# A fused retention and GELU kernel: the written-out order of its 1459 steps is exchanged for another

## Chip, cores and metric

The kernel runs on one core of a Trainium2 chip. The metric is the time of one execution on the device in microseconds (us). Three runs of the kernel before took 286.53, 286.94 and 287.16 us; their median is 286.94. A further execution was profiled.

The core has a matrix engine (PE, with its weight loads shown as PEld), a vector engine (DVE), a scalar engine (ACT), GpSimd (POOL) and a sync engine (SP). Each works through its own list of instructions in order, and semaphores tie the lists together. SP does no arithmetic here: it issues DMAs.

## What is computed

Retention (attention with a causal decay in place of a softmax) over 8 batches, 8 heads, 576 positions and head size 64, then a two-layer network with the tanh form of GELU over the 4608 tokens:

```python
scores = q @ k.transpose(0, 1, 3, 2) / sqrt(64)
rel = pos[:, None] - pos[None, :]
ret = scores * where(rel >= 0, gamma ** rel, 0)   # gamma = 1 - 2 ** (-5 - head)
x = (ret @ v).transpose(0, 2, 1, 3).reshape(4608, 512)
out = gelu_tanh(x @ w_in) @ w_out                 # w_in 512 x 2048, w_out 2048 x 512
```

Inputs and output are float32; the matrix work is done in float16 with sums in float32.

## The kernel before, in words

**Units.** The sequence of a batch is cut into four chunks of 128 positions and a tail of 64, so there are 40 units, u = 5 * batch + chunk. Step `L,u,n` loads q (n = 0), k (1) or v (2) of a unit into a page of SBUF (L227; the tails by two small DMAs, L233; the first two chunks of batches 0 and 1 are loaded as one wide pair, L210 and L215). All pages are loaded by SP. There are 7 sets of pages for units up to 15 and 3 from then on.

Steps `q`, `k`, `v` cast a page to float16, q and v with a factor of decay (L436, wide pairs L451, k by L281 or L279). The last letter names the engine: `v` DVE, `a` ACT, `g` POOL; with no letter q goes to DVE and v to POOL. `D,u` transposes q and k of a unit by one DMA that SP issues (L495). The wide pairs are transposed on PE instead (`t`, L505) and copied out by `y`.

`B,u,w` is the attention's matrix work (lines 541 to 586): it finishes unit w (the earlier state times q at L541, the masked scores times v at L586), and starts unit u (key times value at L565, the scores from the transposed q and k at L575). `m` masks the scores (L703), `a` adds to the running state in float32 (L725, L723), `o` decays it (L733), `z` casts it to float16 in two halves (L281, L279, L743), `Z` zeroes those buffers (L402). `x` moves a finished unit into `xT` (L598 on ACT, L596 on DVE). For wide pairs `X`, `Y`, `R` take the place of `B`.

**The network.** Tokens are taken in 9 blocks t of 512. For blocks 0 to 2 the first layer is `N,t,fc,part` (8 matmuls, L769), followed by `F` (GELU on ACT, L777). For blocks 3 to 8 it is done with 7 instead of 8 products of half-size blocks: `A,t,g,i` (4 matmuls each, L968) for four groups g, with sums of blocks of `xT` (`s`, DVE) and of w_in (`U`, DVE). The products gather in two PSUM banks; `l` copies or adds an intermediate stage out of the bank before the next product adds on top (L279 on ACT, L281 and L829 on DVE), and `f` applies GELU (L986). The second layer of block 0 and of the last 256 tokens is plain (`O`, L795; `P`, L998). All other pairs of 256 tokens use 7 products `W,t,pair,i` (8 matmuls each, L871), with sums of GELU blocks (`H`, DVE) and of w_out (`T`, DVE) and with `V` to carry the results out of PSUM (L829, L279). `e` and `E` copy a plain result, `S` and `Q` store (L787, SP).

The weights are loaded by POOL (`I` for the 8 pieces of w_in, `J` for those of w_out, L250). `K,n` are n filler matmuls (L1014) that write nothing that is read. `g`, `c`, `w` make tables.

**What sets the order.** The steps stand as words in one string, `ORDER`, written out by hand or by a search, and nothing reorders them. A loop at the end of the kernel calls one function per word, and each puts its instructions at the end of the list of its engine:

```python
for step_ in ORDER.split():
    name, *args = step_.split(",")
    do[name](*[int(a) if a.lstrip("-").isdigit() else a for a in args])
```

So the string gives the order on each engine by itself. How two engines run against each other follows at run time from the semaphores, which the framework derives from the tiles that are written and read. Buffers are rings: four for the cast q and k, four for v, four for the transposed pairs, two PSUM banks for the first layer and two for the second.

Of the kernel before, what the change touches and what calls it, by code (L numbers as in the profile page):

```python
# [28 lines left out]
F,1,0,0 N,1,2,0 F,1,2,0 O,0,5 Y,7,0 L,9,1 v,7,v X,7 J,5,g J,4,g Z,0,g O,0,6 J,6,g O,0,7 q,9,g
e,0,1,a F,1,4,0 m,7,0 o,6,1 z,6,1,v O,0,10 O,0,11 e,0,2,a k,9,g a,7,1 z,7,1,g a,8,1 N,1,14,0 D,9 R,7  # L30
B,9,-1 O,0,0 O,0,1 O,0,2 N,1,10,0 O,0,3 O,0,12 O,0,13 T,1,1,v T,2,1,v O,0,14 T,4,1,v F,1,10,0
z,8,1,g F,1,14,0 H,1,0,3,v K,0 x,8 K,0 K,0 T,1,0,v L,10,1 L,10,2 K,0 v,10,v L,11,2 e,0,0,a L,13,1
T,3,0,v x,7 K,0 N,1,2,1 F,1,2,1 k,10,g K,0 L,10,0 q,10,g W,1,0,1 V,1,0,0,a L,11,0 q,11 i,4,v O,0,15
# [1053 lines left out]
```

## Time and profile before

| | before |
|---|---|
| median of 3 runs | 286.94 us (286.53 to 287.16) |
| the profiled execution | 287.18 us |
| its span, first to last instruction | 285.5 us |
| DVE, ACT, POOL busy | 79%, 62%, 41% of the span |
| instructions in the profile | 9676 |
| DMA | 49.77 MB, of which 44.97 MB on SP's queue |

The page says for each engine how long it was busy; the slices cut the span into 40 equal parts, each digit being tenths. "Idle before, releaser" in a row is the time in which the engine waited just before the instruction, and what ended that. A row of the timeline gives start, duration, engine, line, operation, output and inputs, their shape, and a count. A PE row's duration contains the pipeline's drain: starts of successive matmuls, not durations, give PE's pace. For a DMA the row of its issue gives the time that SP took for issuing, and "to landing" the time from the start of the issue until the data is there.

### The profile page before, as it was taken

The page shows a single profiled execution, that of the slowest core. Times are in us where ns is not written, and L with a number is a line of the kernel's source. Part 1 is how long each engine was busy: PE and PEld are TensorE (multiplying, and loading weights), DVE is VectorE, ACT ScalarE, POOL GpSimd, SP SyncE. Part 2 cuts the span into 40 slices and gives each one's busy share as a digit, 9 for nine tenths or more (in the row PEclk, how much of TensorE's full clock was granted, in tenths as well). Part 3 has the DMA queues.
Part 4 walks back from the last instruction along what each step waited for, and adds up shares of the span by engine and source line. Part 5 has one row for each costly group of instructions (what it writes and reads, how often), then busy time and mean ns, then how long its engine had stood idle before and what let it go on. Part 6 is the DMA issues. An engine that isn't in the chain of part 4 may idle for free. (4 is left out here: it accounts for less than half of the span.)

```text
span 285.5 us, 9676 instructions
## 1 busy us (share of the span) xinstructions
PE 275.1 (96%) x4016; PEld 230.7 (81%) x4016; DVE 224.4 (79%) x463; ACT 177.2 (62%) x341; POOL 117.1 (41%) x184
## 2 busy tenths in 40 slices
PE   3999999999999999899999999999999999999995
PEld 1567877568888888888888888888888888888874
DVE  7796273998987789678979998998989986976730
ACT  4265654245576776657777678867777576755611
POOL 5749580525424535392585393707251224000000
DMA  7999999979999999989999989999963521202112
GB/s 223 284 236 257 253 221 182 208 174 190 219 205 199 232 206 163 250 177 202 197 205 248 199 199 172 161 216 210 194 179 76 129 79 54 76 0 77 73 76 73
DMA packets 136427, 49.77 MB, mean 174 GB/s; under 512 B 118208, under 2 KB 130880, under 8 KB 136384
## 3 DMA queue, kind: packets, MB, share of 16 engines
q1 hardware_dynamic: 132032, 44.97, 73.9%
q0 software_dynamic: 4352, 4.20, 9.0%
q8 instruction: 31, 0.51, 0.8%
q14 instruction: 12, 0.10, 0.1%
HBM read 36.70 MB, written 9.44 MB: 162 GB/s over the span
## 5 line engine op out<-in xcount | busy, mean ns | idle before, releaser
L871 PEld LDWEIGHTS <-ssum 128*128 128x128 f16 x480 | 46.8, 98 | 5.5
L769 PE MATMUL bank<-xT,w_in_sb 128*128 128x256 f16 x384 | 47.0, 273 | 0.6 <-DMA w_in_sb<-in_moe_w_in_dram 0.6
L777 ACT ACTIVATE gT<-bank 128x512 f16<-128x512 f32 x48 | 28.3, 597 | 28.5 <-PE bank L769 28.3
L871 PE MATMUL bank<-tsum,ssum 128*128 128x256 f16 x360 | 45.7, 273 | 0.0
L968 PE MATMUL bank<-pages 128*128 128x256 f16 x288 | 42.1, 273 | 0.3 <-ACT pages L279 0.3
L769 PEld LDWEIGHTS <-w_in_sb 128*128 128x128 f16 x384 | 36.3, 98 | 7.2 <-DMA w_in_sb<-in_moe_w_in_dram 1.2
L968 PEld LDWEIGHTS <-pages 128*128 128x128 f16 x384 | 36.6, 98 | 5.4 <-issue 0.7
L871 PEld LDWEIGHTS <-gT 128*128 128x128 f16 x360 | 35.1, 98 | 4.3 <-issue 0.2
L279 ACT COPY hc<-bank 128x512 f32<-128x512 f32 x39 | 22.8, 585 | 23.4 <-PE bank L968 21.4
L436 POOL TENSOR_TENSOR qk<-pages,dec 128x512 f16<-128x512 f32 (+1 forms) x26 | 26.8, 1034 | 21.4 <-PE x L541 7.9
L829 DVE TENSOR_TENSOR hc<-hc,bank 128x512 f32<-128x512 f32 x43 | 29.5, 685 | 6.6 <-PE bank L968 4.3
L281 POOL CAST sz<-s 64x256 f16<-64x256 f32 x42 | 19.1, 454 | 33.5 <-DVE s L725 24.4
L871 PE MATMUL bank<-w_out_sb,gT 128*128 128x256 f16 x240 | 31.1, 273 | 0.0
L968 PEld LDWEIGHTS <-w_in_sb 128*128 128x128 f16 x288 | 27.2, 98 | 3.9 <-issue 0.2
L968 PE MATMUL bank<-xT,w_in_sb 128*128 128x256 f16 x192 | 28.8, 273 | 0.0
L436 POOL TENSOR_TENSOR v<-pages,dec 128x512 f16<-128x512 f32 (+1 forms) x23 | 22.9, 1003 | 12.2 <-PE bank L968 6.1
L986 ACT ACTIVATE gT<-hc 128x512 f16<-128x512 f32 x43 | 26.8, 629 | 1.2 <-DVE hc L829 1.1
L281 POOL CAST qk<-pages 128x512 f16<-128x512 f32 (+1 forms) x22 | 13.7, 631 | 32.1 <-DMA pages<-in_k_dram 19.6
L829 DVE TENSOR_TENSOR ssum<-gT 128x1024 f16<-128x1024 f16 x30 | 23.0, 772 | 1.2 <-ACT gT L777 0.8
L598 ACT ACTIVATE xT<-x 128x512 f16<-128x512 f32 (+1 forms) x38 | 20.5, 546 | 4.9 <-PE x L586 3.8
L829 DVE TENSOR_TENSOR ost<-u,bank 128x256 f32<-128x256 f32 x45 | 18.5, 416 | 6.1 <-PE bank L871 5.8
L279 ACT COPY pages<-bank 128x512 f32<-128x512 f32 x29 | 16.9, 582 | 9.9 <-PE bank L968 9.6
(113 smaller groups left out, 485.9 us busy)
## 6 DMA issues: line engine op xcount, KB each, us to landing
out_dram<-ost SPq DMA_DIRECT2D x35, 256.0 KB, 2.9
pages<-in_q_dram SPq DMA_DIRECT2D x32, 256.0 KB, 4.6
pages<-in_k_dram SPq DMA_DIRECT2D x24, 256.0 KB, 4.4
pages<-in_v_dram SPq DMA_DIRECT2D x24, 256.0 KB, 4.6
pages<-in_k_dram SPq DMA_DIRECT2D x4, 512.0 KB, 9.6
pages<-in_v_dram SPq DMA_DIRECT2D x4, 512.0 KB, 10.0
w_in_sb<-in_moe_w_in_dram POOLq DMA_DIRECT2D x8, 256.0 KB, 8.1
w_out_sb<-in_moe_w_out_dram POOLq DMA_DIRECT2D x8, 256.0 KB, 7.1
```

What stands on the lines that cost most here:

```text
L279: nc.scalar.copy(out=o, in_=i)
L281: (nc.vector if eng == "v" else nc.gpsimd).tensor_copy(out=o, in_=i)
L436: eng.tensor_tensor(out=out, in0=s["raw"][:, i, 0:n], in1=dec[:, i // 2, s["j"], 0:n].unsqueeze(2).to_broadcast([128, n, D]), op=ALU.mult,)
L598: nc.scalar.activation(out=o, in_=i, func=AF.Copy, bias=0.0, scale=1.0)
L769: nc.tensor.matmul(hps[:, i, :], w_in_sb[:, ct, 128 * (fc + i) : 128 * (fc + i) + 128], xT[:, ct, TB * t % XR + lo : TB * t % XR + hi], st ...
L777: nc.scalar.activation(out=gTs[t][:, fc : fc + TB // (hi - lo), lo:hi], in_=h.pop((t, fc, lo)), func=AF.Gelu_apprx_tanh, bias=0.0, scale=1.0,)
L829: (nc.vector if eng == "v" else nc.gpsimd).tensor_tensor(out=out, in0=a, in1=b, op=op)
L871: nc.tensor.matmul(p["ps", bank][:, HN * col : HN * col + HN], a[:, k], b[:, k], start=(k == 0 and i in (1, 6)), stop=(k == HK - 1), skip_ ...
L968: nc.tensor.matmul(p["ps", bank][:, n], w[:, c, 128 * n : 128 * n + 128], x[:, c], start=(n == 0 and c == 0 and i in (1, 2, 5)), stop=(c = ...
L986: nc.scalar.activation(out=gTs[t][:, f : f + 2, o : o + 256], in_=p["ps", 0] if i == 0 else p["c", i], func=AF.Gelu_apprx_tanh, bias=0.0, ...
```

## The change

Only the string differs (it is a line shorter, so that the lines of the changed kernel's code are lower by 1). Both hold 1459 words. Apart from the fillers the words are the same but for the letter of the engine: 104 words have another engine, and nearly all have another place. The fillers go from 36 matmuls to 32, and before the first matrix step of the attention from 17 to 9. In the summary below, counts of words by engine:

| steps | DVE | ACT | POOL |
|---|---|---|---|
| V, results out of PSUM | 83 to 87 | 22 to 18 | |
| z, casts of the state | 4 to 8 | 21 to 19 | 31 to 29 |
| Z, zeroing | 1 to 5 | | 5 to 1 |
| k, cast of k | 6 to 5 | 8 to 13 | 22 to 18 |
| q, cast of q | 10 to 13 | | 26 to 23 |
| v, cast of v | 11 to 12 | | 25 to 24 |
| l, stages out of PSUM | 76 to 77 | 68 to 67 | |
| x, units into xT | 3 to 4 | 37 to 36 | |
| y, copies of transposes | 4 to 5 | 6 to 5 | |
| e, plain results | 0 to 2 | 5 to 3 | |

The diff, cut to the beginning, the places of the transposes of units 12, 14, 18, 20, 21, 22 and 24, the start of block 5, and the end:

```diff
-K,5 L,0,1 L,0,0 q,0 K,3 Z,5,g K,5 K,4 I,1,g k,0,a t,0,k,h t,0,q,h L,2,0 q,2 y,0,k,v Z,3,g L,0,2
-v,0,g g K,4 y,0,q,a Y,0,1 I,0,g L,4,0 q,4 t,2,q,h y,2,q,a m,0,1 I,3,g I,2,g X,0 a,0,1 Z,1,g K,6
...
-W,1,0,7 m,10 B,11,10 x,10 F,1,0,1 D,12 L,18,0 U,2,0 N,1,6,1 v,13,v V,1,0,1,v U,4,1 a,11,0 z,10,1,g
...
-H,1,1,3,v L,16,0 N,2,4,0 D,14 W,1,0,3 F,2,12,0 V,1,0,6,v z,12,1,a L,18,2 N,2,8,0 V,1,1,0,a W,1,1,2
...
-N,2,14,1 D,18 m,16 S,1,0 v,17,g F,2,14,1 W,2,0,1 z,15,1,g B,17,16 V,2,0,0,a V,1,1,4,v o,16,1 a,17,0
...
-v,19,g V,2,0,4,v W,2,1,1 l,3,1,3,v f,3,0,3 A,3,1,7 A,3,1,5 D,20 v,20,g B,20,19 a,20,0 l,3,1,2,a
...
-D,21 H,3,0,3,v W,2,1,2 l,3,2,0,a A,3,2,6 S,1,2 j,4,a l,3,1,5,v f,3,1,2 L,23,1 a,20,1 v,21,g z,20,1,g
...
-D,22 f,3,2,1 v,24,g W,2,1,4 x,20 W,2,1,5 A,3,3,6 l,3,3,1,a A,3,3,2 S,2,0 m,21 B,22,21 L,25,0
...
-f,4,1,0 D,24 A,4,1,5 l,4,1,4,v W,3,0,3 A,4,2,1 l,4,2,0,v W,3,1,2 q,27,g A,4,1,3 l,4,1,5,v D,25
...
-A,4,3,3 z,27,0,g s,5,1 s,5,2 W,4,0,1 A,5,0,6 s,5,3 l,4,3,5,v s,5,4 l,5,0,1,a V,3,1,6,v m,27 v,28,g
-A,5,0,2 L,31,2 V,4,0,0,a L,33,1 A,5,0,7 l,5,0,3,v A,5,0,5 l,5,0,2,a A,5,0,4 f,5,0,0 S,3,2 q,30,g
...
-S,8,0 f,8,2,3 l,8,3,5,v O,8,10 f,8,3,3 P,2 O,8,11 e,8,2,a E,2,v Q,2 P,1 E,1,a P,0 Q,1 E,0,a S,8,2
-Q,0
+L,0,0 Z,2,v K,1 K,1 K,0 K,6 Z,4,v I,0,g Z,5,v I,1,g g K,1 L,0,1 k,0,a K,0 L,2,1 t,0,k,h y,0,k,v K,5
+q,0,g t,0,q,h L,0,2 v,0,g Z,1,v Z,0,v K,3 k,2,v y,0,q,a Y,0,1 X,0 m,0,1 a,0,1 K,7 Y,0,0 Z,3,g I,2,g
+t,2,k,o I,3,g K,1 z,0,1,a w L,2,0 q,2 I,4,g I,5,g I,6,g c t,2,q,h K,3 L,4,0 a,1,1 o,1,1 y,2,q,a
+L,2,2 m,0,0 R,0 y,2,k,v Y,2,0 m,2,0 x,1 x,0 K,4 q,4,g L,5,0 t,4,q,o z,1,1,a L,4,1 L,4,2 N,0,2,0
...
+x,10 L,13,1 V,1,0,1,v k,13,a T,4,1,v k,12,g D,12 z,11,0,a L,13,2 L,15,0 H,1,1,1,v H,1,1,2,v
...
+q,16,g a,13,1 D,14 F,2,12,0 m,13 B,14,13 U,4,1 m,14 L,17,0 q,17 U,3,0 k,16,a L,16,2 v,16,v x,13
...
+D,18 m,16 N,2,8,1 z,16,0,a F,2,10,1 x,15 B,17,16 F,2,8,1 S,1,0 q,19 V,2,0,0,a N,2,2,1 a,17,0 a,17,1
...
+S,1,3 z,17,0,a B,18,17 L,20,2 x,17 H,2,0,4,v W,1,1,3 W,2,0,2 L,22,0 k,20,g F,2,2,1 D,20 L,21,2
+A,3,0,2 v,19,v s,3,1 l,3,0,0,a s,3,2 A,3,0,6 V,1,1,6,v S,1,2 W,2,0,6 v,20,g V,2,0,2,v s,3,3 a,18,0
...
+l,3,2,4,v a,20,1 f,3,2,1 A,3,2,4 f,3,2,0 D,21 V,2,1,1,v k,23,v A,3,2,3 q,23,g V,2,1,3,v v,21,g
...
+D,22 z,20,1,g B,22,21 x,21 A,3,3,7 l,3,3,2,a A,3,3,5 W,2,1,3 f,3,3,1 L,24,2 v,24,g S,2,1 a,22,0
...
+A,4,1,3 z,23,1,g A,4,2,1 W,3,1,2 v,25,g D,24 V,3,0,6,v L,26,1 l,4,1,5,v D,27 A,4,2,2 m,23 l,4,2,0,a
...
+l,5,0,0,a V,3,1,6,v W,4,0,1 f,4,2,2 A,5,0,6 A,5,0,2 l,5,0,1,a l,5,0,3,v f,4,3,3 A,5,0,7 A,5,0,5
+s,5,4 S,3,3 l,5,0,2,a L,32,1 A,5,0,4 L,29,2 V,4,0,0,a H,4,0,2,v f,5,0,0 W,4,0,2 l,5,0,4,v A,5,0,3
...
+V,8,0,4,v i,0,a V,8,0,5,v S,8,1 W,8,0,3 V,8,0,6,v S,8,0 O,8,8 O,8,9 f,8,3,2 f,8,2,2 P,1 E,1,v S,7,3
+O,8,10 O,8,11 e,8,2,v S,8,2 P,0 E,0,a Q,1 P,2 E,2,a Q,0 Q,2
```

More of the change, by code (lines that the diff above doesn't have):

```diff
@@ L29 @@
[L29 to L33, printed above, removed]
-e,0,3,a L,12,2 T,2,0,v L,14,1 L,9,2 K,0 K,0 U,1,1 U,2,1 v,11,v L,11,1 k,11,v N,1,4,1 T,3,1,v D,10
```

198 lines of the change are left out of this document (100 added, 98 removed).

## Prediction

> **What bounds the kernel now.** I read the page's busy times and slices, the waits of the matrix engine, and then the issues on SP's queue.
>
> ```profile
> PE 275.1 (96%) x4016; PEld 230.7 (81%) x4016; DVE 224.4 (79%) x463; ACT 177.2 (62%) x341; POOL 117.1 (41%) x184
> PE   3999999999999999899999999999999999999995
> POOL 5749580525424535392585393707251224000000
> DMA  7999999979999999989999989999963521202112
> ...
> PE sk L565 <- POOL v L436: 0.7, 1, 0.7
> PE sk L575 <- DMA qkT<-qk: 0.3, 1, 0.3
> PE bank L968 <- ACT pages L279: 0.3, 1, 0.3
> ```
>
> The first four lines are the page, the last three all waits of PE from 30 us to the end. PE is busy 96% of the span and after 30 us it stands still for 1.3 us by name. The matrix work is the same multiset of steps after the change, so the time moves only by PE's start-up, by waits like these three, and by the tail. The DMA line says what comes second: 9 in nearly every slice up to two thirds of the span. POOL has room; its slack costs nothing.
>
> SP alone issues the page loads (L227, L233), the transposes of q and k (L495) and the stores (L787), one after the other. The issues of the stretch 60 to 160 us:
>
> ```profile
> pages<-in_q_dram SPq DMA_DIRECT2D x16, 256.0 KB, 4.6
> out_dram<-ost SPq DMA_DIRECT2D x14, 256.0 KB, 2.9
> pages<-in_k_dram SPq DMA_DIRECT2D x14, 256.0 KB, 4.4
> pages<-in_v_dram SPq DMA_DIRECT2D x14, 256.0 KB, 4.7
> pages<-in_q_dram SPq DMA_DIRECT2D x8, 64.0 KB, 4.5
> pages<-in_v_dram SPq DMA_DIRECT2D x6, 64.0 KB, 4.3
> pages<-in_k_dram SPq DMA_DIRECT2D x6, 64.0 KB, 3.3
> qkT<-qk SPq DMA_TRANSPOSE x18, 4.3
> ...
> 100.00:120.00 20.00, 18.92 (x334) 16.87 (x332) 15.86 (x33) 13.10 (x27) 9.13 (x12) 1.00 1.15 198
> 160.00:180.00 20.00, 19.63 (x290) 17.07 (x288) 18.32 (x36) 15.36 (x31) 11.77 (x16) 1.00 1.05 187
> ```
>
> (The stretches' columns: PE, PEld, DVE, ACT, POOL busy, clock, DMA share, GB/s.) DMA share stays over 1.0 while 44 loads of 256 KB, 20 of 64 KB, 14 stores and 18 transposes pass. I count a load or a transpose as 1 and a small load or a store as half: 44 + 10 + 7 + 18 = 79 in 100 us, **1.27 us per place** on SP's queue. So a transpose that stands one load later lands about 1.27 us later, whatever else is rearranged. That is my choice; the other end is 0, if SP has spare time.
>
> **The change part by part.**
>
> *The transposes' places.* I counted, in both lists, what stands ahead of each D step on SP. Most loads moved ahead of transposes: net places ahead of D are +2 for units 12 and 14, +2.5 for 13, +4 for 21, +1 for 22, +5 for 24, +2 for 26, 31, 32 and 33; -2 for 10 and 11, -1 for 19; 0 for 17, 18, 20 and 30. Against that stands the slack of each in the trace. Unit 14 first, then unit 22:
>
> ```profile
> 80.55 2.42 SPq L495 DMA_TRANSPOSE qkT<-qk  x1
> DMA to landing us min/median/max: 5.9/5.9/5.9
> 91.36 0.26 PE L575 MATMUL sk<-qkT 64*64 64x64 f16 x8
> ...
> 125.53 1.27 SPq L495 DMA_TRANSPOSE qkT<-qk  x1
> DMA to landing us min/median/max: 3.1/3.1/3.1
> 129.21 0.30 PE L575 MATMUL sk<-qkT 64*64 64x64 f16 x16
> ```
>
> Unit 14: issued at 80.55, landed 5.9 later (86.45), read at 91.36: 4.9 us of slack. After: 2 x 1.27 = 2.5 goes to the places; and B,14,13 stands four N steps (0.87 us each, 3.5) earlier in PE's order. 4.9 - 2.5 - 3.5 = -1.1: PE would come 1.1 us before its data. Unit 22: landed 128.6, read 129.21: 0.6 of slack, minus one place, -0.7. By the same sum no other unit comes out later than these. They don't add: whoever is late once is late for the rest.
>
> *Waits that go.* Two of before's waits may be absorbed:
>
> ```profile
> 103.65 0.32 PE L575 MATMUL sk<-qkT 64*64 64x64 f16 x16 [0.34 <-DMA qkT<-qk]
> 117.06 0.32 PE L565 MATMUL sk<-v,qk 64*64 64x64 f16 x16 [0.74 <-POOL v L436]
> 163.19 1.25 PE L968 MATMUL bank<-pages 128*128 128x256 f16 x8 [0.29 <-ACT pages L279]
> ```
>
> The first, unit 18's transpose, keeps its place, so it is a fixed time, not a delay: a PE that is late already doesn't wait there (0.34). The second is the cast of v of unit 20, which stood directly ahead of B,20,19 in the list and now stands some 9 matrix steps ahead: I take its 0.74 as gone. The third stays: A,5,0,6, A,5,0,2, A,5,0,7, A,5,0,5, A,5,0,4 follow each other without a W between them in both lists, each waiting for the copy of the bank before. So lateness runs: 1.1 at unit 14, 0.8 after 18, 0.0 after 20, 0.7 at 22, no later term above it. **Net +0.7**; bounds -1.1 (no place costs anything, both waits go) and +1.9 (1.1 and 0.7 with nothing absorbed, 0.1 for the rest).
>
> *Start-up.*
>
> ```profile
> 4.52 5.41 PE L1014 MATMUL bank<-ident 128*128 128x512 f16 x17 [4.52 <-DVE ident L376]
> 7.03 0.90 POOL L250 DMA_DIRECT2D w_in_sb<-in_moe_w_in_dram  x1
> 10.26 1.90 POOL L451 TENSOR_TENSOR wide<-pages,decw 128x1024 f16<-128x1024 f32 x1 [1.79 <-DMA pages<-in_v_dram]
> 12.11 2.19 POOL L250 DMA_DIRECT2D w_in_sb<-in_moe_w_in_dram  x3
> 26.45 3.78 PE L769 MATMUL bank<-xT,w_in_sb 128*128 128x256 f16 x33 [0.35 <-DMA w_in_sb<-in_moe_w_in_dram]
> ```
>
> Seventeen fillers (K) run ahead of the first transpose, now nine: t,0,k can go at about 8.1 instead of 9.8. But q of unit 0 is cast on POOL: 1.90 by the row of its like, behind two issues of w_in that begin when POOL's masks end (6.5), so 8.2 + 1.9 = 10.1 and t,0,q starts at 10.2, as before. The scores of unit 0 then follow at the old time. What moves is w_in: two groups are issued at 6.5 and 7.3 where only one was (7.03), so the groups behind them are issued about one slot (0.7) earlier, and PE's last wait for them (26.45) shrinks. Estimate **-0.6** by 28 us, between -1.4 (both that wait and the fillers' overshoot gone) and +0.7 (the mask of part 0 now stands behind q,2, a,1,1 and o,1,1 on DVE, so R,0 is later). I carry **0** of it: a PE that is 0.6 early waits 0.6 longer for units 14 and 22, whose places on SP don't know of it. Four fillers fewer (0.9 us) are part of this, not a term of their own.
>
> *Engines of casts and copies.* Counted by letter: DVE gets 4 more V, 4 z (two halves each), 4 Z, 3 q, 2 e and one each of v, x, y, l, and loses one k; POOL loses 4 Z, 4 k, 3 q, 2 z, 1 v; ACT gets 5 k and loses 4 V, 2 z, 2 e, 1 each of l, x, y.
>
> ```profile
> L829 DVE TENSOR_TENSOR ost<-u,bank 128x256 f32<-128x256 f32 x45 | 18.5, 416 | 6.1 <-PE bank L871 5.8
> L281 DVE CAST sz<-old 64x256 f16<-64x256 f32 x4 | 1.3, 313 | 0.1
> L436 DVE TENSOR_TENSOR v<-pages,dec 128x512 f16<-128x512 f32 x7 | 5.9, 849 | 0.0
> L436 DVE TENSOR_TENSOR qk<-pages,dec 128x512 f16<-128x512 f32 x4 | 2.7, 683 | 0.0
> L436 POOL TENSOR_TENSOR qk<-pages,dec 128x512 f16<-128x512 f32 x20 | 22.7, 1138 | 21.1 <-PE x L541 7.9 <-PE bank L871 5.9 <-PE sk L565 3.1
> ```
>
> DVE: V 4 x 0.416 = 1.7; z 8 halves x 0.313 = 2.5; Z at the same 0.313 = 1.3; the other eight net steps between 0.42 and 0.85, at 0.6 = 4.8: **+10 us**. POOL loses about as much (q and v alone 4 x 1.138 = 4.6). DVE's stretch of 160 to 180 is busy for 18.32 of 20, so 1.7 us are free. By place in the list, some 5 of the 10 fall between 110 and 200 us, or 1.1 per 20 us: 18.3 becomes 19.4, still under 20. It is cover, barely. I charge **+0.3**, between 0 and +2 (rival below).
>
> The Trainium skill, SBUF — State Buffer, section "SBUF: two separate sides", says that VectorE operations with two SBUF inputs and GpSimd share a port pair as an exclusive lock. The rows fit: the cast of v means 849 on DVE where that of q, by the same tiles, means 683. By that rule fewer casts on POOL would give DVE part of its 10 us back, and the charge would be 0 instead of 0.3.
>
> *Tail.*
>
> ```profile
> 280.57 0.27 ACT L279 COPY ost<-bank 128x128 f32<-128x128 f32 x1 [0.35 <-PE bank L998]
> 282.27 0.37 ACT L279 COPY ost<-bank 128x256 f32<-128x256 f32 x1 [1.44 <-PE bank L998]
> ```
>
> P,0 (256 columns) was last, now P,2 (128) is: its copy is 0.27 instead of 0.37 and its store 64 KB instead of 128. **-0.2**, at worst 0, if its store queues behind that of P,0.
>
> Sum: +0.7 + 0 + 0.3 - 0.2 = +0.8. The profiled execution took 287.18 (span 285.5), so 288.0; it lay 0.24 above the median of the runs, so the forecast is 286.94 + 0.8 = **287.7**.
>
> **Rivals.** *Faster: SP has spare time.* SP's largest wait from 60 to 180 us, and a row of later fillers for the last rival:
>
> ```profile
> SPq L495 <- POOL v L436: 7.8, 7, 1.4
> ...
> 17.59 1.47 PE L1014 MATMUL bank<-ident 128*128 128x512 f16 x6
> ```
>
> If a place costs under 0.5 us (the moved loads may run in those 7.8 us), units 14 and 22 are in time, and start-up carries: -0.6 - 0.34 - 0.74 - 0.2 = -1.9, less 0.3 for DVE: 285.3 to 286.0. For it: slack of 4 to 6 us at many units. Against: DMA share over 1.0. Chance 0.32.
>
> *No change:* what start-up gives is waited away at SP, and nothing more: 286.9. Chance 0.11.
>
> *DVE becomes the bound.* It has 1.7 us free in 160 to 180; if the 10 us fall unevenly, A steps wait for l, and W for the sums H. It decides from about 1.7 us more per 20; price +2: 288.9. For it: the wait at 163.19 sits where DVE is fullest. Chance 0.17.
>
> *The clock.* The first 17 fillers took 5.41, 0.32 each, six later ones 1.47, 0.25 each: the early ones run slower. With nine ahead instead of 17, matrix work could fall into that slow time; if the 1.5 us of it between 8 and 13 us took twice as long, +1.5: 288.4, less what start-up gives. The Trainium skill, TensorE: Matmul & The Clock Gate, section "What's actually happening", has the clock fall after a window of some 3.4 us idle; no gap of that length is left. Chance 0.04.
>
> **How the numbers follow.** The forecast has 0.36 and its own range 287.2 to 288.6. A measurement of this kernel tells about 0.2%, 0.57 us, from no change (286.37 to 287.51). Of the forecast's 0.36, 0.05 lie within that: same 0.05 + 0.11 = 0.16; faster 0.32; slower 0.31 + 0.17 + 0.04 = 0.52. The range goes from the faster case's 285.2 to 289.8 (transposes at +1.9 and some DVE): 0.8.
>
> **What would show it.** Right: PE waits at L575 for DMA qkT around units 14 (about 88 us) and 22 to 24, 0.5 to 1.2 us together; no wait of L565 for v of unit 20; the wait at A,5,0 as before; transposes with 0 to 1 us of slack where before had 4. Wrong: those transposes land with 2 us to spare; PE's first N steps start over 1 us early and stay so; or PE waits for DVE at L871 and L968 instead. A stall at a load of a v or k page would be something that I have not priced.

## The result and the profile after

The changed kernel took 290.48 us, the median of four runs (289.87 to 290.94); the kernel before took 287.05 beside it (286.53 to 287.33). The ratio is 1.012, with a 95% interval of 1.0094 to 1.0147: 3.4 us slower. Slower was forecast as the likeliest, but by 0.8 us, and the time lies above the range. On another chip the changed kernel took 1.0062 (1.0018 to 1.0106) of the kernel before; its scatter is part of the story below. Ratios leave out executions more than 1.5% above the fastest of their kernel, among them the profiled ones of two experiments (one step ahead on POOL, the old letters).

The page after, with the lines that answer to those shown of before:

```profile
PE 274.9 (95%) x4012; PEld 230.2 (80%) x4012; DVE 231.8 (80%) x487; ACT 175.1 (61%) x333; POOL 108.3 (38%) x168
...
PE   3799999999999999889999999999999999999995
...
POOL 5882380404052733734075525526741214000000
DMA  6999999999999899999999799999775510301022
```

PE is as busy as before (274.9 us against 275.1) in a span of 288.5 us instead of 285.5. Its row has two 8s, from 115 to 130 us, where before had one. All waits of PE from 30 us on, after the change (total, times, longest):

```profile
PE x L540 <- POOL sz L742: 1.1, 1, 1.1
PE bank L967 <- ACT hc L278: 1.0, 1, 1.0
PE bank L967 <- DVE hc L828: 0.7, 3, 0.3
PE bank L967 <- DVE pages L828: 0.4, 1, 0.4
```

Not one of them names a transpose (DMA qkT), which the prediction put first. The waits named come to 3.2 us where before had 1.3.

**Where the 3.0 us lie.** Matmuls are pipelined, so I took every start-to-start time of two successive matmuls in both traces, subtracted the median of its kind (109 ns for 256 columns, 216 for 512, and so on), and added up what is left; this is the loss. The traces are up to 3 us out of step, so the stages are cut at steps ahead of which both orders have done the same matrix work, and not at equal times:

| stage of the matrix work | ends at, before and after (us) | loss before | loss after | difference |
|---|---|---|---|---|
| the first 22 matrix steps | 28.0, 28.4 | 6.52 | 7.81 | +1.29, less 0.86 for 4 fillers fewer: +0.43 |
| to W,1,1,3 | 104.5, 104.5 | 7.24 | 6.88 | -0.36 |
| to A,4,0,1 | 133.1, 135.0 | 2.41 | 4.28 | +1.87 |
| to A,5,0,6 | 161.9, 163.9 | 2.17 | 2.23 | +0.06 |
| to A,6,1,1 | 193.1, 196.1 | 2.89 | 3.84 | +0.95 |
| to PE's last start | 282.0, 285.2 | 3.44 | 3.71 | +0.27 |
| from there to the end | 285.5, 288.5 | 3.51 | 3.23 | -0.28 |

That is 2.94. The last matmul, whose own pace is in neither sum, has 128 columns before and 256 after; with its 0.05 us it is the 3.0 by which the span grew. (The losses of the start contain the fillers' slow early pace.) Two stages carry most of it: from W,1,1,3 to A,4,0,1, about 105 to 135 us, and from A,5,0,6 to A,6,1,1, about 162 to 196 us.

**From 105 to 135 us: casts that wait for pages, and what stands behind them.** Two rows of PE, then POOL's and ACT's rows ahead of the two large waits, all of the changed kernel (start, us, engine, line, operation; in brackets the idle time just before and what ended it):

```profile
117.61 0.29 PE L540 MATMUL x<-qkT,sz 128*128 128x64 f16 x4 [1.08 <-POOL sz L742]
...
124.27 1.03 PE L967 MATMUL bank<-pages 128*128 128x256 f16 x8 [1.02 <-ACT hc L278]
```

```profile
106.63 0.61 POOL L280 CAST qk<-pages 128x512 f16<-128x512 f32 x1 [4.02 <-DMA pages<-in_k_dram]
113.15 1.04 POOL L435 TENSOR_TENSOR v<-pages,dec 128x512 f16<-128x512 f32 x1 [5.91 <-PE bank L967]
114.14 0.61 POOL L280 CAST qk<-pages 128x512 f16<-128x512 f32 x1
114.70 1.04 POOL L435 TENSOR_TENSOR qk<-pages,dec 128x512 f16<-128x512 f32 x1
115.70 1.85 POOL L742 TENSOR_TENSOR sz<-s,gend 64x256 f16<-64x256 f32 x2
```

```profile
121.24 0.63 ACT L985 ACTIVATE gT<-pages 128x512 f16<-128x512 f32 x1
123.11 0.62 ACT L278 CAST qk<-pages 128x512 f16<-128x512 f32 x1 [1.25 <-DMA pages<-in_k_dram]
123.64 0.58 ACT L278 COPY hc<-bank 128x512 f32<-128x512 f32 x1
```

POOL: the cast of v of unit 20 waits 5.91 us. The row names a PE bank, but the load of that page was issued at 108.78 and landed at 113.01, so it is the page; a releaser that had long been done is no releaser. Behind this cast stand k,21 and q,21 and only then z,18,1, whose input had been ready, and which B,20,19 on PE waits for: 1.85 us to 117.55, and PE starts at 117.61. ACT is the same picture: the cast of k of unit 22 waits for its page until 123.1, and the copy l,3,2,1 that empties PE's bank stands behind it.

Where that page went is seen on SP. Its issue, before and after (in each group of two it is the first, then the second):

```profile
101.85 1.14 SPq L227 DMA_DIRECT2D pages<-in_k_dram  x2
```

```profile
116.33 2.67 SPq L226 DMA_DIRECT2D pages<-in_k_dram  x2
```

Before, the page landed at 105.4 and was cast at 121.0, with over 15 us of slack. Now it lands at 123.0 and its cast is late.

**The transposes.** Units 14 and 22 in the changed kernel, issue, landing, and PE's reading matmul:

```profile
L494 SPq DMA_TRANSPOSE qkT<-qk x1: 1794/1794/1794, 82.2 to 82.2; - x1
...
DMA to landing us min/median/max: 5.2/5.2/5.2
```

```profile
L574 PE MATMUL sk<-qkT x8: 192/203/213, 88.5 to 88.5; 64*64 64x64 f16 x8
```

```profile
L494 SPq DMA_TRANSPOSE qkT<-qk x1: 2135/2135/2135, 125.8 to 125.8; - x1
...
DMA to landing us min/median/max: 4.3/4.3/4.3
```

```profile
L574 PE MATMUL sk<-qkT x16: 192/193/193, 131.1 to 131.3; 64*64 64x64 f16 x16
```

82.2 + 5.2 = 87.4, read at 88.5: 1.1 us of slack where before had 4.9. 125.8 + 4.3 = 130.1, read at 131.1: 1.0 where before had 0.6. The slack did shrink at unit 14, by 3.8 us, and it grew a little at unit 22; neither was late.

**From 162 to 196 us.** The stretch of 160 to 195 us before and after (PE, PEld, DVE, ACT, POOL busy, clock, DMA share, GB/s), and three waits of the changed kernel:

```profile
160.00:195.00 35.00, 34.63 (x521) 30.46 (x519) 32.23 (x64) 25.86 (x52) 17.69 (x26) 1.00 1.04 191
```

```profile
160.00:195.00 35.00, 34.00 (x560) 29.66 (x559) 33.18 (x68) 27.25 (x55) 14.32 (x21) 1.00 0.99 195
```

```profile
164.75 0.60 PE L967 MATMUL bank<-xT,w_in_sb 128*128 128x256 f16 x4 [0.30 <-DVE hc L828]
...
166.19 0.60 PE L967 MATMUL bank<-pages 128*128 128x256 f16 x4 [0.41 <-DVE pages L828]
...
183.78 0.60 PE L967 MATMUL bank<-xT,w_in_sb 128*128 128x256 f16 x4 [0.15 <-DVE hc L828]
```

DVE has 0.95 us more to do here and ACT 1.4, and POOL 3.4 less; PE waits for copies out of its banks. The larger loss from A,5,0,6 to A,6,1,1 comes back in every trace: it is 2.89 us in the trace of before and in three experiments that keep its order there (the new head, the new tail, page 22 late), 3.84 in the trace of the changed kernel, and 3.61 to 4.64 in twelve further traces of the changed order with the full loads. The waits that have a name do not all come back: the first two, at A,5,0,2 and A,5,0,5, stand in four of these thirteen traces. In this pair the largest differences lie ahead of the products A,5,1,7 (0.27 us), A,6,0,6 (0.22), A,5,3,2 (0.19) and those of A,5,0 (0.18 together).

**Tail**, ACT's last rows:

```profile
284.62 0.37 ACT L278 COPY ost<-bank 128x256 f32<-128x256 f32 x1 [6.84 <-PE bank L997]
285.47 0.27 ACT L278 COPY ost<-bank 128x128 f32<-128x128 f32 x1 [0.48 <-DMA out_dram<-ost]
```

The narrow copy is last, as predicted, and the end comes 3.23 us after PE's last start instead of 3.51.

### The profile page after: what moved, and what is told of

Read it like the earlier page. It is cut to its first block, busy times and chain, and to the rows that moved or that the text cites. A ratio compares the mean times of both kernels' runs of the same rounds, so it can differ in the third digit from the quotient of the medians.

```text
span 288.5 us, 9665 instructions
## 1 busy us (share of the span) xinstructions
PE 274.9 (95%) x4012; PEld 230.2 (80%) x4012; DVE 231.8 (80%) x487; ACT 175.1 (61%) x333; POOL 108.3 (38%) x168
## 4 chain that ended last, share of the span: by engine, by line
PE 80%; DMA 7%; DVE 5%; SPq 4%; ACT 3%; issue 1%; DVEq 0%; ACTq 0%
PE bank L870 27%; PE bank L967 22%; PE bank L768 15%; PE bank L794 6%; DMA pages<-in_q_dram 4%; PE x L540 2%; DMA pages<-in_k_dram 2%; PE sk L564 2%; DVE hc L828 1%; PE sk L574 1%; SPq L214 1%; SPq L226 1%; SPq L209 1%; PE x L585 1%; PE x L688 1%
## 5 line engine op out<-in xcount | busy, mean ns | idle before, releaser
L967 PE MATMUL bank<-pages 128*128 128x256 f16 x288 | 42.1, 273 | 1.6 <-ACT hc L278 1.0
L967 PEld LDWEIGHTS <-pages 128*128 128x128 f16 x384 | 36.6, 98 | 6.9 <-issue 2.0
L280 POOL CAST sz<-s 64x256 f16<-64x256 f32 x34 | 16.7, 491 | 47.7 <-DVE s L724 26.9
L967 PEld LDWEIGHTS <-w_in_sb 128*128 128x128 f16 x288 | 27.6, 98 | 4.5 <-issue 1.0
L967 PE MATMUL bank<-xT,w_in_sb 128*128 128x256 f16 x192 | 28.8, 273 | 0.7 <-DVE hc L828 0.7
L435 POOL TENSOR_TENSOR qk<-pages,dec 128x512 f16<-128x512 f32 (+1 forms) x22 | 22.0, 1000 | 17.5 <-PE sk L564 9.7
L435 POOL TENSOR_TENSOR v<-pages,dec 128x512 f16<-128x512 f32 (+1 forms) x22 | 21.0, 960 | 19.5 <-PE bank L967 9.1
L828 DVE TENSOR_TENSOR pages<-pages,bank 128x512 f32<-128x512 f32 x29 | 19.8, 683 | 4.8 <-PE bank L967 4.4
L828 DVE TENSOR_TENSOR ssum<-gT,ssum 128x1024 f16<-128x1024 f16 x30 | 22.4, 748 | 0.3
```

What stands on the lines that cost most here:

```text
L280: (nc.vector if eng == "v" else nc.gpsimd).tensor_copy(out=o, in_=i)
L435: eng.tensor_tensor(out=out, in0=s["raw"][:, i, 0:n], in1=dec[:, i // 2, s["j"], 0:n].unsqueeze(2).to_broadcast([128, n, D]), op=ALU.mult,)
L828: (nc.vector if eng == "v" else nc.gpsimd).tensor_tensor(out=out, in0=a, in1=b, op=op)
L967: nc.tensor.matmul(p["ps", bank][:, n], w[:, c, 128 * n : 128 * n + 128], x[:, c], start=(n == 0 and c == 0 and i in (1, 2, 5)), stop=(c = ...
```

## Experiments

Theory "queue": casts that wait for late pages hold up, in in-order queues, short steps that PE needs. Rivals: "transposes" (the prediction's step, lying underneath), "DVE" (its load), "start-up". Diffs are of words of the list; a ratio is that of a kernel to the kernel before on the same chip, with its 95% interval. The chips differ, and the changed kernel itself came to 1.012 on one and 1.0062 on another; so a difference of 0.006 between two ratios below shows nothing by itself.

### One step ahead on POOL

```diff
 W,2,0,6
-v,20,g
 V,2,0,2,v
...
 a,18,1
+z,18,1,g
+v,20,g
...
 m,19
-z,18,1,g
 B,20,19
```

> The changed kernel (290.48 us) with two POOL steps exchanged: the cast of the state of unit 18, second half (z,18,1), goes directly behind the addition that it reads (a,18,1) and so ahead of the cast of v of unit 20, behind which it stood in POOL's queue. Theory 'queue' (a cast that waits for a late page holds up, in an in-order queue, work whose data is there): PE's wait of 1.1 us at L540 for POOL's sz goes and stays gone, 290.5 - 1.1 = 289.4. Rival 'transposes' (my prediction's step: the transposes, on SP, set PE's time underneath): unit 22's transpose landed 0.64 us before it was read, so only 0.6 is gained and PE then waits at L574 for DMA qkT: 289.9. Rival 'DVE' (the 10 us more of work on DVE cost the time): the wait comes back at the next bank copy, 290.5.

Ratio 1.0115 (1.0047 to 1.0183). PE's wait for sz L742 is gone in this trace, but the profiled execution took 294.02, the longest of six (288.30 to 294.02): page 22 landed later, at 125.5 instead of 123.0, and the wait behind its cast became 3.8 us.

```profile
125.55 0.62 ACT L278 CAST qk<-pages 128x512 f16<-128x512 f32 x1 [4.01 <-DMA pages<-in_k_dram]
```

```profile
126.70 1.12 PE L967 MATMUL bank<-pages 128*128 128x256 f16 x8 [3.78 <-ACT hc L278]
```

So in this execution one wait was mended and the next took more than the gain. There is no wait at L574, so "transposes" isn't what lies underneath here.

### The cast of k,22 one step later on ACT

```diff
 L,22,1
-k,22,a
 A,3,2,6 l,3,2,1,a
+k,22,a
 V,2,1,2,a
```

> The changed kernel with the cast of k of unit 22 on ACT moved one ACT step later, behind the bank copy l,3,2,1. Theory 'queue': the cast waited for its page until 123.11 and the copy behind it held PE up by 1.18 us at 124.27; the wait goes: 289.4 to 289.5. Rival 'transposes': 0.6 at most, 289.9, with a wait of PE at L574 for unit 22. Rival 'DVE': 290.5.

Ratio 1.0102 (1.0067 to 1.0136); the profiled execution took 288.25, without either wait: page 22 landed at 120.5 and POOL was done with z,18,1 in time. It was the shortest of nine; the others, 288.6 to 295.2, suggest luck with the landings rather than the edit alone.

### Both moves

```diff
-v,20,g
...
 a,18,1
+z,18,1,g
+v,20,g
...
-k,22,a
 A,3,2,6 l,3,2,1,a
+k,22,a
```

> Both moves (z,18,1 ahead on POOL, the cast of k of unit 22 behind l,3,2,1 on ACT). Theory 'queue': the two waits are separate and add, 290.5 - 1.1 - 1.1 = 288.3. Rival 'transposes': the slack of unit 22 (0.64) and of unit 21 (1.16) is used up, 289.8, and PE waits at L574. Rival 'DVE': 290.5.

Ratio 1.0112 (1.0056 to 1.0168): the waits did not add up to a gain. In the trace the page landed late again, and the wait came back at the step that now stands behind the cast, the copy V,2,1,2 to ost:

```profile
125.76 0.62 ACT L278 CAST qk<-pages 128x512 f16<-128x512 f32 x1 [1.90 <-DMA pages<-in_k_dram]
126.28 0.36 ACT L278 COPY ost<-bank 128x256 f32<-128x256 f32 x1
```

```profile
126.70 1.03 PE L870 MATMUL bank<-tsum,ssum 128*128 128x256 f16 x8 [1.75 <-ACT ost L278]
```

A place one step later only changes the name of the wait while the page is later than that.

### The old letters in the new order

```diff
-k,22,a
+k,22,v
...
-z,10,0,g
+z,10,0,a
```

and so for all 104 words.

> The changed kernel's order with the engine letter of every step as it was in the kernel before (104 words). DVE gives back its 7 us more of busy time and the cast of k of unit 22 goes back to DVE. Theory 'queue' (z,18,1 keeps its letter and place, k,22 leaves ACT): the wait at 124.27 goes (-1.1), that at 117.61 stays; 289.4. Theory 'DVE' (the load on DVE is the cost): the small waits for DVE at 164 to 167, 183 and 214 us (0.3 + 0.6 + 0.3 + 0.3) go too, 288.0 to 288.5. Rival 'order' (the places alone cost the time, letters nothing): 290.5, or slower, since the places were found with the other letters: up to 292.

Ratio 1.0746 (1.0691 to 1.0801), over 20 us slower, which no theory had. PE waits 5.2 us for the w_out weights, which POOL issues between its casts, and at a dozen places for copies. DVE's load was lower than after the change (225.9 us busy against 231.8) and the time far longer, so load alone is no measure; an order and its letters belong together.

### The old head

```diff
-L,0,0 Z,2,v K,1 K,1 K,0 K,6 Z,4,v I,0,g Z,5,v I,1,g g K,1 L,0,1 k,0,a
...
+K,5 L,0,1 L,0,0 q,0 K,3 Z,5,g K,5 K,4 I,1,g k,0,a t,0,k,h t,0,q,h
...
```

> The changed kernel with its first 93 words (up to the scores of unit 4) in the order, with the letters and with the 36 fillers of the kernel before; the rest as changed. In the traces the changed kernel does the same matrix work 0.8 to 1.1 us later from 25 us to 70 us. Theory 'start-up carries' (what is lost at the start stays lost): 290.5 - 0.9 = 289.6. Rival 'start-up is waited away' (the pages that come late set PE's time at 115 to 125 us whatever came before; the lead had shrunk to 0.3 by 95 us): 290.2 to 290.5, and PE's waits at 117 and 124 us get longer by what the start gave.

Ratio 1.0082 (1.0045 to 1.0119). The trace speaks for neither: PE is as late at 30 us as with the new head, because groups of w_in that now stand behind the seam (where the exchanged words meet the others) come late (two waits, 1.0 us), and at 124 us it waits 2.9 us behind the cast of k,22. A head can't be cut off cleanly here.

### The k page of unit 22 three loads earlier on SP

```diff
 l,3,0,1,a
+L,22,1
 L,22,2 A,3,0,7
...
 v,20,g
...
 m,20
-L,22,1
 k,22,a
```

> The changed kernel with one load moved on SP: the k page of unit 22 (L,22,1) goes ahead of L,22,2, L,23,0 and L,23,1, three loads earlier; no cast is moved. Theory 'late page' (1.27 us per place on SP holds for loads as I used it for transposes): the page lands 3 us earlier, the cast on ACT that waits for it starts when ACT comes to it, and the wait of up to 1.2 to 3.9 us at the bank copy behind it goes: 290.5 - 1.2 = 289.3, and the slow runs of 292 and more go with it. Rival 'places cost nothing' (SP's order doesn't matter, the page comes when the DMA engines have room): it lands at the same time and the time stays 290.5. Rival 'transposes': gain 0.6, then PE waits at L574.

Ratio 1.0074 (1.0037 to 1.0111). The profiled execution took 287.33, and neither large wait is in it. One execution can't say what the place does, so I count over all traces of the changed order: where the page kept its late place and the cast stood ahead of l,3,2,1 (the changed kernel twice, the kernels with z,18,1 moved, the old head, and q,0 on DVE), PE waited 1.0, 0.9, 3.8, 2.9 and 0.7 us at L967 for ACT's hc there; in the sixth such trace, with six letters put back, PE came to that product over 2 us later and didn't wait there. Where the page came earlier (four kernels), none waited at that place. For z,18,1: with its old place PE waited 1.1, 1.2, 1.2 and 2.2 us in four traces and not in four others; with its new place, in none of four. With the rows shown above, both waits are thus seen to hang on what stands behind a late page. In this trace the stage from W,1,1,3 to A,4,0,1 lost 1.81 us, against 4.28 after the change and 2.41 before. A gain over all executions isn't shown, as the changed kernel has 1.0062 elsewhere.

### Six letters put back between 155 and 192 us

```diff
-q,28
+q,28,g
...
-z,27,1,v
+z,27,1,g
```

and V,4,0,2 to ACT, v,30, k,32 and q,32 to POOL.

> The changed kernel with six letters between 155 and 192 us put back as before: the casts q,28, v,30, k,32, q,32 and z,27,1 to POOL, V,4,0,2 to ACT, 4.0 us less on DVE there. Theory 'DVE is the bound' between 160 and 190: PE's waits at L967 for DVE's hc and pages (0.46, 0.57, 0.31, 0.23 more than the usual pace) go, 290.5 - 1.0 = 289.5. Rival 'POOL takes its place' (casts that wait for pages stand ahead of others in POOL's queue): the waits change their names, 290.5 or later. Rival 'A,5 stays' (A,5,0,7 to A,5,0,4 follow each other too closely, as before): 0.3 to 0.5 goes, 290.1.

Ratio 1.0139 (1.0083 to 1.0195). DVE's busy time from 160 to 195 us fell from 33.18 to 30.52, and the loss from A,5,0,6 to A,6,1,1 did not fall: 4.38 against 3.84. Waits changed their names, as the second rival had it. Of these two, the first is the known one for z,18,1, at 119.6 us, and the second lies at 179 us, for z,27,1 on POOL:

```profile
PE x L540 <- POOL sz L742: 2.2, 1, 2.2
PE x L540 <- POOL sz L280: 0.6, 1, 0.6
```

### All in one

```diff
+K,5 L,0,1 L,0,0 q,0 K,3 Z,5,g K,5
...
 a,18,1
+z,18,1,g
+v,20,g
...
+L,22,1
 L,22,2 A,3,0,7
...
+q,28,g
```

> All in one: the old head, z,18,1 ahead of v,20 on POOL, the k page of unit 22 three loads earlier, six letters put back. If the parts are independent and as large as the traces say: 290.5 - 0.9 - 1.1 - 1.2 - 1.0 = 286.3, 0.2% below the kernel before (the rest is the tail's 0.26). Theory 'waited away': the start-up and DVE terms give nothing, 288.2. Theory 'transposes': 289.5 with PE waiting at L574 for units 21, 22 and 16 (slack 0.6 to 0.9).

Ratio 1.0107 (1.0071 to 1.0142): nothing gained. Both mended waits are gone, and PE waits 1.2 us at L574 for unit 18's transpose at 105.7 us, the first time in the changed order that one is late. Then 0.6 us for z,27,1 as above.

### The old head and the page alone

```diff
+K,5 L,0,1 L,0,0 q,0 K,3 Z,5,g K,5
...
+L,22,1
 L,22,2 A,3,0,7
```

> The changed kernel with the old head and with the k page of unit 22 three loads earlier on SP, the two edits that helped when made alone (1.0082 and 1.0074 of the kernel before, where the changed kernel is 1.012). If they are independent they add: 1.0036, about 1.0 us over the kernel before, and what is left are the waits for DVE and the products that follow each other too closely between 150 and 215 us. Rival 'waited away' (pages set the time at 105 to 125 us whatever comes earlier): 1.007 to 1.008, as with the page alone, and a wait at L564 or L574 near 105 us.

Ratio 1.0099 (1.0063 to 1.0135): they don't add. The rival was right, down to the place:

```profile
106.15 0.32 PE L574 MATMUL sk<-qkT 64*64 64x64 f16 x16 [1.44 <-DMA qkT<-qk]
```

From about 100 to 125 us pages and transposes come in one queue with the DMA engines' share at 1.0 or more. What is mended in front of one is waited for at the next.

### The new head on the kernel before

```diff
-K,5 L,0,1 L,0,0 q,0 K,3 Z,5,g K,5 K,4 I,1,g k,0,a t,0,k,h t,0,q,h
...
+L,0,0 Z,2,v K,1 K,1 K,0 K,6 Z,4,v I,0,g Z,5,v I,1,g g K,1 L,0,1 k,0,a
...
```

> The kernel before with the first 93 words of the changed kernel (its order, letters and fillers), the rest as before. Theory 'start-up carries': + 0.8 us over the kernel before (1.003). Rival 'waited away' (before's own waits at 103 and 117 us, 0.34 and 0.74, shrink by as much): 0 to + 0.2. My prediction's estimate for these 93 words was -0.6: 0.998.

Ratio 1.0104 (1.0074 to 1.0134), slower than any of the three. The seam is at fault again: PE waits 0.7 us for a cast of unit 5 at 26.8 us and 0.8 us for xT at 29.9 us, which neither parent has. It tells one thing: PE came to unit 20 1.7 us later than in the kernel before, and the wait for its v was still there, with 0.9 us instead of 0.74. My prediction had taken such waits for fixed in time, and shrinking by what PE is late.

### The new tail on the kernel before

```diff
-P,2 O,8,11 e,8,2,a E,2,v Q,2 P,1 E,1,a P,0 Q,1 E,0,a S,8,2 Q,0
+P,1 E,1,v S,7,3 O,8,10 O,8,11 e,8,2,v S,8,2 P,0 E,0,a Q,1 P,2 E,2,a Q,0 Q,2
```

> The kernel before with its last 14 words as in the changed kernel: the last products P in the order 1, 0, 2 where they were 2, 1, 0, so that the last copy and store have 128 columns instead of 256. Theory (my prediction's step): -0.2 us, 0.9993. Rival (the store queues behind the one before it): 0. In the traces, from PE's last matmul to the end of the span: before 3.5 us, changed 3.3 us; the profiled execution of this kernel should show 3.3.

Ratio 0.9994 (0.9975 to 1.0014). The interval is wider than the term. In the trace the end comes 3.2 us after PE's last start (282.2 of 285.4), where before had 3.5, so the term is there and is too small to time.

### The k page of unit 22 late in the kernel before

```diff
 z,16,1,g
-L,22,1
 B,18,17
...
 f,3,1,2
+L,22,1
 L,23,1
```

> The kernel before with one load moved on SP: the k page of unit 22 (L,22,1) goes from ahead of L,20,1 to directly ahead of L,23,1, past five other loads, three transposes (units 19, 20, 21) and two stores, each of which comes one place earlier. A test of the price of a place. Theory '1.27 us per place': v of unit 20 lands 1.27 us earlier, so that PE's wait of 0.74 for it at 117 us goes, and the time is 0.7 us under the kernel before (0.9975); page 22 itself lands at about 120 us, 1 to 2 us ahead of its cast. Rival 'places cost nothing': the landings stay within 0.4 us of before and the time is the same. Rival 'page 22 late': its cast on DVE waits and holds the copies behind it up, + 0.5 us or more.

Ratio 0.9989 (0.9956 to 1.0023): the same. The price of a place holds in the trace, but only as a mean: of eleven loads and transposes that moved up one place, the landings came 0.3 to 2.6 us earlier, 1.5 on average (the trace stood 0.4 us later just ahead of them). It is a rough mean: in the trace with the new tail, which has the order of before here, landings of the same stretch came up to 0.9 us earlier without any move. The wait for v of unit 20 is gone, as expected, but it is absent with the new tail too, so the move isn't shown to be the cause; another, at 104 us for unit 18's transpose, took 0.6. The late page did no harm here: it landed at 120.4, when DVE came to its cast.

### The changed kernel again

> The changed kernel once more, for its scatter beside the others: 289.9 to 290.9 in four runs so far. If late pages set the time, this execution's waits near 117 and 124 us differ from the 1.1 and 1.0 us seen (0 to 3.8), and those further back (0.46 at A,5,0,2, 0.31 at A,5,3,2, 0.3 at A,6,3,2) come back to 0.05.

Ratio 1.0062 (1.0018 to 1.0106); twelve executions from 287.79 to 292.27. The profiled one took 291.2 and has the same waits at 118.4 and 124.9 us (1.2 and 0.9).

### Lighter loads, in both orders

```diff
+            g = H // 2 if u >= 10 else H
             nc.sync.dma_start(
-                out=r[:, n],
-                in_=src[b, :, 128 * c : 128 * c + 128, :].rearrange("h s d -> s h d"),
+                out=r[:, n, 0:g],
+                in_=src[b, 0:g, 128 * c : 128 * c + 128, :].rearrange("h s d -> s h d"),
             )
```

The casts read the four heads twice, by a view, with the same number of elements.

> The kernel before with half of the bytes in each load of q, k and v from unit 10 on (four heads of eight are loaded, and the casts read these four twice; the tails are loaded whole). Its output isn't the reference's. Theory 'late pages': before loses only 0.35 to 0.8 us to pages and transposes (at 103 and 117 us): 286.3. Rival 'DMA nowhere': 287.4, as before.

> The changed kernel with the same lighter loads; its output isn't the reference's. Theory 'late pages': its waits near 117 and 124 us go and its scatter shrinks to that of the kernel before; what is left over g1 is start-up 0.8, DVE and ACT 1.4, less 0.3 of tail: 1.9 us over g1, 288.2. Rival 'pages are all of it': within 0.3 us of g1. Rival 'pages are nothing': 3.4 over g1, as without the lighter loads.

The changed order: 288.47 us, ratio 1.0018 (0.9987 to 1.0049), twelve executions from 287.85 to 289.48. The waits at 117 and 124 us are gone and so is two thirds of the scatter. Against 289.76 us of the changed kernel on the same chip that is 1.3 us, in all. In the two traces the stage from W,1,1,3 to A,4,0,1 lost 1.67 us instead of 4.32, and the stage from A,5,0,6 to A,6,1,1 lost 4.85 instead of 3.87. So by these traces the late pages cost more than 1.3 us, and the lighter loads took some of it back elsewhere.

The order of before: 289.98 us, ratio 1.0077 (1.0037 to 1.0116). It became slower, against both theories. The wait for v of unit 20 is gone, and this stands in its place, a wait for a sum on DVE:

```profile
PE bank L883 <- DVE ssum L841: 1.7, 1, 1.7
```

DVE and POOL just before it, with lighter loads (L841 is the line of the sums, L441 that of the casts):

```profile
131.62 2.07 DVE L841 TENSOR_TENSOR pages<-xT,pages 128x512 f16<-128x512 f16 x2
133.62 1.09 DVE L841 TENSOR_TENSOR ssum<-gT 128x1024 f16<-128x1024 f16 x1
134.75 1.41 DVE L841 TENSOR_TENSOR ssum<-gT,ssum 128x1024 f16<-128x1024 f16 x1
```

```profile
131.19 2.23 POOL L441 TENSOR_TENSOR qk<-pages,dec 128x512 f16<-128x512 f32 x2 [2.42 <-DMA pages<-in_q_dram]
133.37 0.80 POOL L282 CAST qk<-pages 128x512 f16<-128x512 f32 x1
134.14 1.48 POOL L441 TENSOR_TENSOR v<-pages,dec 128x512 f16<-128x512 f32 x1
```

Before, those sums took 0.95 (two), 0.69 and 0.69, and POOL's casts began at 134.62, behind them. With earlier pages the casts run beside the sums, and these sums take 1.6 to 2.2 times as long. The stage from A,4,0,1 to A,5,0,6 lost 3.96 us instead of 2.17.

### Two casts from POOL to DVE, with lighter loads

```diff
 l,3,3,5,v
+q,26
+q,25
...
-q,26,g
...
-q,25,g
```

> The kernel before with lighter loads (289.98 us; its output isn't the reference's) and two casts moved from POOL to DVE, q of units 26 and 25, to directly behind l,3,3,5 and so behind the sums H,3,0,1 and H,3,0,2. DVE gets 1.4 us of work more. Theory 'DVE's f16 sums slow down beside POOL' (0.69 us with POOL idle, up to 1.5 beside it): the sums near 134 us come back from 1.09 and 1.41 towards 0.69, s,4,2 and s,4,4 from 2.07 towards 0.95, and PE's wait of 1.9 at 136 us shrinks to 0.9 or less: 288.8 to 289.0. Rival 'DVE has too much work there': the wait stays and 0.5 to 1.4 comes on top later: 290.5 or more.

289.0 us against 289.98 on another chip; ratio 1.0067 (1.0045 to 1.0088), where without the move it was 1.0077 (1.0037 to 1.0116). The busy engine got 1.3 us more to do, and PE's wait for the sum shrank from 1.74 to 0.70 us, as the theory said:

```profile
131.02 1.32 DVE L841 TENSOR_TENSOR pages<-xT,pages 128x512 f16<-128x512 f16 x2
132.26 1.52 DVE L841 TENSOR_TENSOR ssum<-gT 128x1024 f16<-128x1024 f16 x1
133.82 0.69 DVE L841 TENSOR_TENSOR ssum<-gT,ssum 128x1024 f16<-128x1024 f16 x1
```

```profile
131.45 0.61 POOL L282 CAST qk<-pages 128x512 f16<-128x512 f32 x1 [3.29 <-PE bank L980]
132.02 1.22 POOL L441 TENSOR_TENSOR v<-pages,dec 128x512 f16<-128x512 f32 x1
```

The sum that still has POOL beside it takes 1.52, the one that no longer has takes 0.69. But PE now waits for a copy on DVE soon after:

```profile
137.03 1.03 PE L883 MATMUL bank<-tsum,ssum 128*128 128x256 f16 x8 [0.54 <-DVE u L841]
```

The stage from A,4,0,1 to A,5,0,6 lost 3.61 us instead of 3.96: a gain of 0.35. The two profiled executions lie 0.65 us apart, but 0.69 us of smaller loss at the start are part of that. So it is shown that the sums slow down beside POOL; that the move made the kernel 1.0 us faster is not.

### q of unit 0 on DVE

```diff
-q,0,g
+q,0
```

> The changed kernel with one letter put back: q of unit 0 is cast by DVE, as before, and not by POOL, where it stands ahead of the cast of v that PE's first product X,0 waits for. Theory 'start-up carries': PE's waits of 0.45 at L647 and 0.58 at L630 shrink and the time falls by 0.5 to 0.8: 289.8. Rival 'waited away': PE is up to 0.8 earlier at 25 us, and no earlier at 130 us: 290.5.

Ratio 1.0069 (1.0031 to 1.0107), as the changed kernel. The wait of the first product for POOL is gone, and the second transpose waits 0.69 us for q instead, whose cast now stands behind the copy y,0,k on DVE. This letter alone is not what the start costs.

### Seven steps moved

```diff
 a,18,1
+z,18,1,g
+v,20,g
...
+L,22,1
 L,22,2 A,3,0,7
...
-o,26,1 H,4,0,1,v
 A,4,3,3 l,4,3,5,v
+o,26,1 H,4,0,1,v
...
 A,5,3,1
+l,5,2,5,v
 l,5,3,0,a a,30,0
...
 A,5,3,3 l,6,0,0,a
+z,30,1,a
...
 A,6,2,3
+l,6,2,5,v
```

> The changed kernel with seven steps moved and no letter changed: z,18,1 ahead of v,20 on POOL; the k page of unit 22 three loads earlier on SP; on DVE l,4,3,5 ahead of o,26,1 and H,4,0,1, l,5,2,5 ahead of a,30,0, and l,6,2,5 directly behind its product; on ACT l,6,0,0 ahead of z,30,1. Theory 'order of the queues' (each wait is a short step standing behind another in an in-order queue): the waits at 118, 125, 165, 184, 191 and 215 us go: 289.8 to 290.5 less 1.1, 1.0, 0.4, 0.3, 0.2, 0.3 = 286.5 to 287.2. Rival 'waited away' (as when head and page were mended together: a wait for a transpose came up near 105 us): the three on DVE and ACT go, the others change their names: 289.

Ratio 1.0066 (1.0028 to 1.0103), executions from 286.8 to 292.45. The waits at 118, 125 and 184 us are gone from the trace; others, each a loss of 0.7 us, stand at 128 and 189 us, that at 215 us stays (0.23), and the loss from A,5,0,6 to A,6,1,1 is 4.19. The wait at 189 us, at A,6,0,6, stands in the trace of "the cast of k,22 one step later" as well, without any reorder there. No kernel tried beats the kernel before by more than its interval.

## Why the prediction was wrong

**Transposes: +0.7 forecast, 0 found.** The step failed. By the sum unit 14's slack was to fall by 6.0 us, from 4.9 to -1.1; it fell by 3.8, to 1.1. Two places made its landing 0.9 us later (87.4 instead of 86.45) and not 2.5, and PE read it 2.9 us earlier and not 3.5. At unit 22 PE itself came 1.9 us later, and the slack grew from 0.6 to 1.0. So a price per place, even if its mean is near the forecast (1.5 in the test, 1.27 in the sum), doesn't give the landing of one transfer.

**Pages: no term, +1.87 found** from W,1,1,3 to A,4,0,1. The prediction counted places on SP for transposes only. What it left out is that loads were moved back too, that a cast waits for its page, and that a whole queue waits for the cast. For the k page of unit 22 a sum of the same kind would have done: issued 16 us later, it has used up its 15 us of slack. The prediction named this case at its end, "a stall at a load of a v or k page", and gave it no price. The two waits took 1.08 and 1.02 us, where before had 0.34 and 0.74 in this stage.

**Waits that go.** Unit 18's 0.34 and v of unit 20's 0.74 did go in this pair. Why isn't settled: of the order of before, the trace with the new tail has no wait for v of unit 20 either. That such waits go because PE is late already, with fixed times on SP, is not borne out: with PE 1.7 us late (the new head on the kernel before) the wait for v of unit 20 stayed, as its page landed at 110.75 us instead of 108.83.

**The wait at A,5,0 stays:** right in kind, but it grew: 0.30 at A,5,0,2 and 0.41 at A,5,0,5 after, 0.29 at A,5,0,7 before.

**Start-up: 0 carried, +0.43 found** in this pair. My reading of w_in was right in part: PE's two waits for it, 0.29 and 0.35 us, went. But PE waited at its first scores, at X,0 and at R,0 (0.45, 0.58 and 0.43 us) for a copy, a cast and the mask instead. Eight traces of the changed order with these 93 words and the full loads lose 7.0 to 8.9 us here, three of the order of before 6.5 to 6.9; the means, 8.0 and 6.7, differ by 0.5 us beyond the fillers' 0.86. That q of unit 0 sits on POOL isn't the cause by itself.

**DVE: +0.3 forecast, +0.95 found** from A,5,0,6 to A,6,1,1; this term was mis-sized. I had compared sums per stage, 19.4 of 20 us, and called that cover. The sum itself was near (DVE was busy for 19.32 us from 160 to 180 us; over the whole span it got 7.4 us more and not 10). But in the rows shown PE doesn't wait for a sum of work, it waits for single copies out of its banks. The rival "DVE becomes the bound" had +2 and named this place, though its mechanism isn't borne out: 2.7 us less work on DVE from 160 to 195 us didn't make the loss smaller (4.38 against 3.84), nor did another order of steps on DVE and ACT (4.19) or the old letters in the new order (4.54). That points to the places of the steps rather than to the engines they run on, but no edit shows it. Which steps cost the 0.95 us stays open.

The Trainium skill, SBUF — State Buffer, section "SBUF: two separate sides", says that the port pair which VectorE and GpSimd share is an exclusive lock for a whole instruction. The prediction set a charge of 0 beside its 0.3 by it. The traces fit the rule in kind: beside each other, sums of DVE took up to 1.42 us instead of 0.69 and a cast of v on POOL 1.48 instead of 1.04, which doesn't tell a lock from a sharing. They don't fit that use: POOL had 8.8 us less to do, and the loss on DVE's side grew all the same. Where one of DVE's sums meets POOL's casts counts, as the lighter loads show, and not only how many casts POOL has.

**Tail: -0.2 forecast, -0.28 found.** Right.

**The clock** played no part between the two profiled executions; both show 1.00 in all stretches quoted.

In the end the sum of +0.8 had 0.7 for transposes that were in time, nothing for the pages (1.9), 0.3 instead of 0.95 for DVE, and nothing for the start (0.4); the stages without a term came to 0.0 together (-0.36, +0.06 and +0.27). The chance of the faster case was too high: it rested on the slack of transposes, and no other transfer's slack had been looked at.

## What to carry to other kernels

In a list written out by hand, look for the slack of every transfer, not of one kind: for each load, landing against the cast that reads it, and then what stands behind that cast on its engine. Two traces that are out of step are compared between points of equal work, not of equal time. A cast that may wait belongs behind the short steps that the matrix engine needs next. An order that was found on one pattern of landings fits that pattern: pages that come earlier can cost as much as pages that come later, because casts then meet other work.

## What the runs showed of the hardware

**DVE's float16 sums beside POOL.** Of the 60 sums of GELU blocks (`H`, 128x1024 float16) in the trace of before, 38 have no POOL instruction beside them: mean 0.686 us, at most 0.693. Of 15 with POOL beside them for over half of their time the mean is 0.955, the longest 1.42, and the shortest 0.68, no longer than alone. Moving two casts off POOL brought one of them back to 0.69.

**A stalled PE can come back at half pace.** In the kernel with z,18,1 moved, around its wait of 3.8 us (columns as above; the clock stands behind POOL):

```profile
122.80:126.70 3.90, 0.12 (x2) 0.00 (x0) 0.98 (x1) 1.15 (x3) 1.88 (x2) 1.00 0.63 120
126.70:131.00 4.30, 4.30 (x25) 3.22 (x25) 2.02 (x5) 2.34 (x5) 0.62 (x1) 0.60 0.98 195
131.00:135.00 4.00, 4.00 (x90) 3.58 (x87) 3.16 (x7) 2.92 (x7) 2.39 (x4) 1.00 0.88 215
```

From 127.6 to 130.8 us matmuls of 256 columns start 213 ns apart instead of 109, which costs another 1.6 us. After waits of 2.9 us (the old head) and 2.2 us (six letters put back) the same happened, for 2.9 and 3.2 us, and after 5.0 us (the old letters) the granted clock was 0.50 for 6.8 us; after 1.75 us (both moves) and 1.74 us (lighter loads in the order of before) it did not. So a long wait costs more than its length. The Trainium skill, TensorE: Matmul & The Clock Gate, section "What's actually happening", has the clock fall after an idle window of about 3.4 us; here 2.2 us were enough once. My rival on the clock had looked for such gaps at the start only.

**The spread of one kernel.** The mean time from issue to landing of the full pages between 60 and 125 us differs from execution to execution, 4.31 to 4.93 us in twelve traces of the changed order and its variants with the full loads. The three with the shortest (4.31, 4.37 and 4.37: page 22 early, k,22 later, seven steps moved) took 287.33, 288.25 and 288.38 us, the one with the longest (4.93, both moves) 291.92. What makes the landings differ isn't shown.
